# The fifth and sixth chunk loaded earlier, and the dense copies of v made by the scalar engine

## The chip, the cores and the metric

The kernel runs on one core of a Trainium2 chip. The core has a matrix engine (PE, with its weight loads shown as PEld), a vector engine (DVE), a scalar engine (ACT), GpSimd (POOL) and a queue processor (SP) that issues DMA transfers here. Each works through its own instructions in program order, and they wait for each other through semaphores. The metric is device time in microseconds for one run of the kernel; lower is better. Before the change it is 358.11 us, the median of three runs (357.58 to 358.33).

## The reference, cut to what matters

```python
# q, k, v: (8, 8, 576, 64) = batch, head, position, head dimension
scores = q @ k^T / 8                                  # per batch and head
D[n, m] = gamma_h ** (n - m) if n >= m else 0         # gamma_h = 1 - 2 ** (-5 - h)
ret = (scores * D) @ v                                # no softmax
x = ret.transpose(0, 2, 1, 3).reshape(4608, 512)      # tokens by heads
gate = sigmoid(x @ w_gate);  val = x @ w_val          # (4608, 1536) each
out = (gate * val) @ w_out                            # (4608, 512)
```

It is a causal attention with a decay in place of the softmax, so that it can be computed chunk by chunk with a running state; a gated feed-forward layer follows on the same tokens. All inputs are 32-bit floats; the kernel works in bf16 with 32-bit accumulation.

## The kernel before, in words

The 576 positions of a batch are cut into four chunks of 128 and one of 64. A chunk of one batch is a step: 40 in all, numbered from 0, and steps 4, 9, 14 and so on are the half ones. Steps 0 to 3 (the first batch without its tail) take a special path by pairs and read their own loads (`load_pair`). From step 4 on every step goes the same way:

- `load(s)`: three DMA loads on SP, for v, k and q, in pieces of 256 bytes.
- `casts_to(s)`: GpSimd (POOL) scales k and q by the decay tables and casts them to bf16. k goes into `kbd`, a block diagonal tile (three buffers, four instructions for a full chunk), q into `qs` (one instruction). `cross(s)` puts two DMA transposes on SP, k to `kT` and q to `qT`. `cast_v` then writes v to `vbd`, block diagonal, in four copies and, where the chunk isn't the last of its batch, to `vs`, a dense copy, in four more (L252).
- Phase "qk": PE multiplies `kT` and `qT`, and DVE applies the causal mask.
- Phase "pv": PE multiplies scores with `vbd` and adds q times the state, and ACT copies the result, as xT, into the input of the feed-forward part.
- Phases "st0" and "st1": PE multiplies `kbd` and `vs`, which updates the state; DVE casts the state for the next half chunk.

The feed-forward part takes the tokens in blocks of 128 to 512. For each of twelve slices of the hidden layer (an h unit) PE computes gate and value (L457) in PSUM tiles with three buffers, ACT takes the sigmoid, and DVE multiplies. Then PE multiplies by `w_out` (L520), ACT copies the result to an `ob` tile of four, and SP stores it. The attention phases of later steps are spread between these units by `advance`; `run_phase("qk", s)` also issues the loads of step s + 5 and the casts of step s + 2.

All loads share one pool of 18 buffers of 256 KB. SP issues in the order in which the program is written. Every load and transpose counts up one of eight semaphores in turn, and its issue waits for the transfer eight places earlier, so that at most eight are in flight.

The start is written out by hand. SP has pair 0, weights, pair 1, weights (`load_w(f, nf)` loads gate and value weights of nf slices from f), then steps 4 and 5, then `w_out` (`load_wo`). POOL, ACT and DVE cast the weights to bf16 (`cast_w`, `cast_wo`), in the order of the lines around L619 to L660; `h_first(...)` runs the h units of the first block between them. The first multiplication by `w_out` (L664) takes three token tiles at once and has the phases of steps 4 and 5 inside it.

Of the kernel before, what the change touches and what calls it, by code (L numbers as in the profile page):

```python
# [10 lines left out]
BF16 = mybir.dt.bfloat16  # L11
# [5 lines left out]
def kernel(  # L17
# [19 lines left out]
    nc = tc.nc  # L37

    B, H, S, D = q.shape
    NT, DM = out.shape  # L40
    DFF = moe_w_gate.shape[1]
    P = 128
    M = H // 2
    NC = (S + P - 1) // P
    NKC = DM // P
    NFC = DFF // P
# [3 lines left out]
    nat_pool = ctx.enter_context(tc.tile_pool(name="nat", bufs=4))  # L50
# [14 lines left out]
    STEPS = [(b, c) for b in range(B) for c in range(NC)]  # L65
    width = [min(P, S - c * P) for c in range(NC)]
    first_tok = [b * S + c * P for (b, c) in STEPS]
    NS = len(STEPS)
# [3 lines left out]
    loaded = {}  # L72
    parts = {}

    def load(s):
        b, c = STEPS[s]
        n = width[c]
        t0 = c * P
        tiles = []
        for nm, src in (("v", v), ("k", k), ("q", q)):  # L80
            t = ld_pool.tile([P, H, D], FP32, tag="ld", name=f"{nm}32_{s}")
            nc.sync.dma_start(out=t[0:n], in_=src[b, :, t0:t0 + n, :].rearrange("h p d -> p h d"))
            tiles.append(t)
        loaded[s] = tiles
# [11 lines left out]
    def load_w(f, nf):  # L96

        for nm, src in (("g", moe_w_gate), ("v", moe_w_val)):
            for i in range(nf):
                r = NKC // nf  # L100
                t = ld_pool.tile([P, r, nf * P], FP32, tag="ld", name=f"w{nm}32_{f}_{i}")
                nc.sync.dma_start(
                    out=t, in_=src[i * r * P:(i + 1) * r * P, f * P:(f + nf) * P].rearrange("(c p) f -> p c f", p=P))
                parts[nm, f, i] = t

    def load_wo(f):
        t = ld_pool.tile([P, DM], FP32, tag="ld", name=f"wo32_{f}")
        nc.sync.dma_start(out=t, in_=moe_w_out[f * P:(f + 1) * P, :])
        parts["o", f] = t
# [3 lines left out]
    load_pair(1)  # L113
    load_w(2, 2)
    load_w(4, 4)
    load_w(8, 4)
    load(4)
    load(5)
    for f in range(5):
        load_wo(f)  # L120
    LEAD_LOAD = 5
    LEAD_CAST = 2
# [68 lines left out]
    def cast_w(nm, f, nf, i, eng):  # L191
        r = NKC // nf
        at = (slice(None), slice(i * r, (i + 1) * r), slice(f * P, (f + nf) * P))
        eng(out=(wg_sb if nm == "g" else wv_sb)[at], in_=parts.pop((nm, f, i)))  # L194

    on_pool, on_act, on_dve = nc.gpsimd.tensor_copy, nc.scalar.copy, nc.vector.tensor_copy
# [7 lines left out]
    natural = {}  # L204
# [36 lines left out]
    def cast_v(s):  # L241

        b, c = STEPS[s]
        n = width[c]
        v32 = loaded[s][0]
        vb = vbd[s % NB]
        vs = nat_pool.tile([P, 2, M, D], BF16, tag="vs", name=f"vs_{s}")
        for j in range(n // 64):
            for hh in range(2):
                nc.gpsimd.tensor_copy(out=vb[half(hh), j, :, half(hh)], in_=v32[half(j), hh::2, :])  # L250
                if c < NC - 1:
                    nc.gpsimd.tensor_copy(out=vs[half(hh), j], in_=v32[half(j), hh::2, :])  # L252
        natural["vb", s] = vb
        natural["vs", s] = vs

    def cross(s):

# [18 lines left out]
    def half(x):  # L276
        return slice(x * 64, x * 64 + 64)
# [46 lines left out]
    def tile_sv(s, eng):  # L324
        sb = sbd[s % 4]
        for hh in range(2):
            eng(out=sb[half(hh), :, half(hh)], in_=st_tiles[STEPS[s][0]][half(hh)])
        state[s, 1] = sb
# [28 lines left out]
    def phase_qk(s):  # L357
        n = width[STEPS[s][1]]
        nj = n // 64
        kT, qT = turned["k", s], turned["q", s]  # L360
        pt = att_pool.tile([P, M, P], BF16, tag="pt", name=f"pt_{s}")
        qkp = qk_psum.tile([P, M, P], FP32, tag="qk", name=f"qk_{s}")
        for j in range(nj):
            for m in range(M):
                nc.tensor.matmul(qkp[:, m, half(j)], lhsT=kT[:, j, m, :], rhs=qT[:, m, half(j)],  # L365
                                 start=True, stop=True)
        nc.vector.tensor_tensor(out=pt[:, :, 0:n].rearrange("p m (j t) -> p m j t", t=64),  # L367
                                in0=qkp[:, :, 0:n].rearrange("p m (j t) -> p m j t", t=64),
                                in1=tri.unsqueeze(1).unsqueeze(1).to_broadcast([P, M, nj, 64]), op=ALU.mult)
        probs[s] = pt  # L370

    def phase_pv(s):
        b, c = STEPS[s]
        n = width[c]
        t0 = first_tok[s]
        qT = turned["q", s]
        pt = probs.pop(s)
        vb = natural["vb", s]
        pvp = pv_psum.tile([P, M, P], FP32, tag="pv", name=f"pv_{s}")
        for j in range(n // 64):  # L380
            before = state.get((s, j - 1) if j else (s - 1, 1)) if c or j else None
            for m in range(M):
                if before is not None:
                    nc.tensor.matmul(pvp[:, m, half(j)], lhsT=before[:, m, :], rhs=qT[:, m, half(j)],  # L384
                                     start=True, stop=False)
                nc.tensor.matmul(pvp[:, m, half(j)], lhsT=vb[:, j, m, :], rhs=pt[:, m, half(j)],  # L386
                                 start=before is None, stop=True)
        nc.scalar.copy(out=xT[:, :, t0:t0 + n], in_=pvp[:, :, 0:n])  # L388
# [29 lines left out]
    def loads_to(s):  # L418
        while done["ld"] <= min(NS - 1, s):
            load(done["ld"])  # L420
            done["ld"] += 1

    def casts_to(s):
        while done["cast"] <= min(NS - 1, s):
            x = done["cast"]
            cast_k(x)
            cast_q(x)
            cross(x)
            cast_v(x)
            done["cast"] += 1  # L430

    def run_phase(kind, s):
        if kind == "qk":
            loads_to(s + LEAD_LOAD)
            casts_to(s + LEAD_CAST)
            phase_qk(s)
        elif kind == "pv":
            phase_pv(s)
        else:
            phase_st(s, int(kind[2]))  # L440

# [105 lines left out]
    def run(units):  # L547
        for _ in units:
            tick()
# [4 lines left out]
    def h_first(fcs, a, e):  # L554
        run(h_units(gvs, fcs, 0, a, e))
# [63 lines left out]
    pair_out(1, 1, on_dve)  # L619
    pair_st(1, 1)  # L620
    tile_sv(3, on_act)
    for f in (4, 8):
        for i in range(4):
            cast_w("g", f, 4, i, on_pool)
    h_first((2, 3), 0, 2 * P)
    for i in range(2):
        nc.vector.memset(vbd[i], 0.0)
    casts_to(4)
    for f in range(5, 10):
        load_wo(f)  # L630
    casts_to(5)
    for f in range(10, NFC):
        load_wo(f)
    loads_to(6)
    h_first((0, 1, 2), 2 * P, 4 * P)
# [5 lines left out]
    cast_w("v", 4, 4, 3, on_dve)  # L641
    nc.vector.memset(vbd[3], 0.0)
    h_first((4, 5), 0, 4 * P)
    cast_w("v", 8, 4, 0, on_act)
    h_first((6,), 0, 4 * P)
    cast_w("v", 8, 4, 1, on_act)
    cast_w("v", 8, 4, 2, on_dve)
    h_first((7,), 0, 4 * P)
    cast_w("v", 8, 4, 3, on_act)
    h_first((8, 9), 0, 4 * P)  # L650
    cast_wo(0, on_dve)
    cast_wo(1, on_act)
# [70 lines left out]
```

## Time and profile before

| | |
|---|---|
| median of 3 runs | 358.11 us (357.58 to 358.33) |
| the profiled execution | 358.44 us, of which 356.7 us is the span of the profile |
| PE busy | 333.6 us (94%) |
| DVE busy | 162.1 us (45%) |
| ACT busy | 126.8 us (36%) |
| POOL busy | 225.9 us (63%) |
| mean granted PE clock | 0.981 |
| dense copies of v on POOL (L252) | 112 x 399 ns = 44.7 us |

The span runs from the first to the last instruction of one execution; all times inside it are counted from its start. Busy is the time in which an engine has an instruction under way, without its waits. The granted clock is the share of full speed that PE's clock had. In a timeline a row has its start, its length, engine, line, operation, what is written and read, and the number of instructions; square brackets give the idle time before it and what ended it. Such a releaser is inferred from the semaphores: where an instruction waits for several, the one named came last, and if the engine named had long been done, it was another, often a DMA. Rows with "SPq" are issues of transfers, not the transfers.

### The profile page before, as it was taken

The numbers are of one execution on the slowest core, as the hardware profiler recorded it, in microseconds if no ns is written. First come the engines' busy times: TensorE is split into PE (matmuls) and PEld (weight loads), VectorE is DVE, ScalarE is ACT, GpSimd is POOL, SyncE is SP. The second block draws the span as 40 slices with busy tenths as digits, with TensorE's granted clock in tenths as the row PEclk, the third lists the DMA queues.
The fourth block names the chain that finished last, engine by engine and source line by source line (L and its number), as shares of the span: only waits on it lengthen the run. The fifth ranks groups of instructions, "written<-read, shape, count | busy, mean of one in ns | idle before, by whom it ended". The sixth has DMA issues, their size and how long they took to land.

```text
span 356.7 us, 7632 instructions
## 1 busy us (share of the span) xinstructions
PE 333.6 (94%) x2833; PEld 192.2 (54%) x2868; DVE 162.1 (45%) x343; ACT 126.8 (36%) x245; POOL 225.9 (63%) x447
## 2 busy tenths in 40 slices
PE   7899977967699999999999999999999999999996
PEld 3574434755575665655655655555455545554443
DVE  5656412534364653651644663653456345512420
ACT  6766302312233333434323423332333234333321
POOL 7442978999974999489853999879649990000000
PEclk9999989969989999999999999999999999999999
DMA  7999999999999999983985999999699550011002
GB/s 221 315 378 247 230 297 166 207 218 212 189 188 196 209 154 235 208 142 123 179 173 142 163 191 209 197 180 188 145 166 194 130 115 12 0 61 59 2 25 93
DMA packets 169396, 60.27 MB, mean 169 GB/s; under 512 B 152848, under 2 KB 161296, under 8 KB 169360
## 3 DMA queue, kind: packets, MB, share of 16 engines
q1 hardware_dynamic: 169216, 59.66, 82.9%
q8 instruction: 22, 0.36, 0.4%
q14 instruction: 14, 0.11, 0.1%
q10 hardware_dynamic: 144, 0.13, 0.1%
HBM read 37.75 MB, written 9.44 MB: 132 GB/s over the span
## 4 chain that ended last, share of the span: by engine, by line
PE 72%; POOL 14%; DMA 7%; issue 3%; DVE 2%; ACT 1%; SPq 1%; POOLq 0%; ACTq 0%; DVEq 0%
PE h L457 41%; PE op L520 21%; POOL kbd L227 6%; POOL vbd L250 3%; POOL vs L252 2%; POOL qs L237 2%; DMA qT<-qs 2%; DMA q<-in_q_dram 2%; PE qk L365 2%; PE st L398 2%; PE pv L386 2%; PE pv L384 2%; DMA k<-in_k_dram 1%; DMA q32p<-in_q_dram 1%; DVE sbd L404 1%
## 5 line engine op out<-in xcount | busy, mean ns | idle before, releaser
L457 PE MATMUL h<-xT,wv_sb 128*128 128x512 bf16 (+3 forms) x585 | 119.1, 325 | 0.8 <-DVE wv_sb L194 0.4
L457 PE MATMUL h<-xT,wg_sb 128*128 128x512 bf16 (+3 forms) x584 | 119.0, 326 | 0.3
L227 POOL TENSOR_TENSOR kbd<-k,ktab 64x256 bf16<-64x256 f32 x128 | 78.3, 612 | 47.4 <-PE st L398 32.7
L484 DVE TENSOR_TENSOR gv<-g,h 128x512 bf16<-128x512 bf16 (+1 forms) x104 | 65.1, 626 | 69.1 <-PE h L457 65.0
L480 ACT ACTIVATE g<-h 128x512 bf16<-128x512 f32 (+1 forms) x104 | 57.0, 548 | 95.9 <-PE h L457 79.4
L520 PE MATMUL op<-wo_sb,gv 128*128 128x512 bf16 x356 | 84.1, 379 | 0.8
L457 PEld LDWEIGHTS <-wg_sb 128*128 128x128 bf16 x592 | 53.1, 100 | 35.7 <-issue 0.3
L457 PEld LDWEIGHTS <-wv_sb 128*128 128x128 bf16 x592 | 53.1, 100 | 33.3 <-DVE wv_sb L194 0.9
L367 DVE TENSOR_TENSOR pt<-qk,tri 128x512 bf16<-128x512 f32 (+1 forms) x36 | 22.7, 630 | 72.0 <-PE qk L365 71.7
L520 PEld LDWEIGHTS <-gv 128*128 128x128 bf16 x372 | 34.4, 98 | 36.3
L404 DVE CAST sbd<-st 64x256 bf16<-64x256 f32 x112 | 47.0, 420 | 14.9 <-PE st L398 12.5
L250 POOL CAST vbd<-v 64x256 bf16<-64x256 f32 x128 | 50.7, 396 | 4.4
L252 POOL CAST vs<-v 64x256 bf16<-64x256 f32 x112 | 44.7, 399 | 0.0
L492 ACT COPY ob<-op 128x512 f32<-128x512 f32 x35 | 20.3, 587 | 66.3 <-PE op L520 53.6
L237 POOL TENSOR_TENSOR qs<-q,qtab 128x512 bf16<-128x512 f32 (+1 forms) x36 | 37.5, 1041 | 2.8
L388 ACT CAST xT<-pv 128x512 bf16<-128x512 f32 (+1 forms) x36 | 19.4, 538 | 30.2 <-PE pv L386 30.1
L365 PE MATMUL qk<-qT,kT 128*128 128x64 bf16 x256 | 13.6, 195 | 10.4 <-DMA qT<-qs 10.4
L365 PEld LDWEIGHTS <-kT 128*128 128x128 bf16 x256 | 12.7, 99 | 17.1 <-DMA kT<-kbd 9.2
L470 ACT ACTIVATE g<-h 128x256 bf16<-128x256 f32 x32 | 12.3, 384 | 25.3 <-PE h L457 24.2
L398 PEld LDWEIGHTS <-kbd 128*128 128x128 bf16 x224 | 13.5, 100 | 13.2 <-DVE sbd L404 5.1
L386 PE MATMUL pv<-pt,vbd 128*128 128x64 bf16 x256 | 19.5, 194 | 0.0
L384 PE MATMUL pv<-qT,sbd 128*128 128x64 bf16 x228 | 18.5, 195 | 0.1
(66 smaller groups left out, 177.9 us busy)
## 6 DMA issues: line engine op xcount, KB each, us to landing
out_dram<-ob SPq DMA_DIRECT2D x35, 256.0 KB, 2.2
v<-in_v_dram SPq DMA_DIRECT2D x28, 256.0 KB, 3.6
k<-in_k_dram SPq DMA_DIRECT2D x28, 256.0 KB, 4.4
q<-in_q_dram SPq DMA_DIRECT2D x28, 256.0 KB, 5.0
wg<-in_moe_w_gate_dram SPq DMA_DIRECT2D x12, 256.0 KB, 5.6
wv<-in_moe_w_val_dram SPq DMA_DIRECT2D x12, 256.0 KB, 5.5
wo<-in_moe_w_out_dram SPq DMA_DIRECT2D x12, 256.0 KB, 4.0
k32p<-in_k_dram SPq DMA_DIRECT2D x4, 256.0 KB, 4.6
```

The source lines that it names most:

```text
L227: nc.gpsimd.tensor_tensor(out=kn[half(hh), j, :, half(hh)], in0=k32[half(j), hh::2, :], in1=ktab[half(j), c, hh::2].unsqueeze(2).to_broadc ...
L237: nc.gpsimd.tensor_tensor(out=qs[0:n], in0=q32[0:n], in1=qtab[0:n, c, :].unsqueeze(2).to_broadcast([n, H, D]), op=ALU.mult)
L250: nc.gpsimd.tensor_copy(out=vb[half(hh), j, :, half(hh)], in_=v32[half(j), hh::2, :])
L252: nc.gpsimd.tensor_copy(out=vs[half(hh), j], in_=v32[half(j), hh::2, :])
L365: nc.tensor.matmul(qkp[:, m, half(j)], lhsT=kT[:, j, m, :], rhs=qT[:, m, half(j)], start=True, stop=True)
L384: nc.tensor.matmul(pvp[:, m, half(j)], lhsT=before[:, m, :], rhs=qT[:, m, half(j)], start=True, stop=False)
L386: nc.tensor.matmul(pvp[:, m, half(j)], lhsT=vb[:, j, m, :], rhs=pt[:, m, half(j)], start=before is None, stop=True)
L404: nc.vector.tensor_copy(out=sb[half(hh), :, half(hh)], in_=st_tiles[b][half(hh)])
L457: nc.tensor.matmul(out, lhsT=w_sb[:, kc, fc * P:(fc + 1) * P], rhs=xT[:, kc, t0 + a:t0 + e], start=(kc == 0), stop=(kc == NKC - 1))
L480: nc.scalar.activation(out=g[:, 0:n], in_=h1[:, 0:n], func=AF.Sigmoid)
L484: nc.vector.tensor_tensor(out=gvs[some[0]][:, a:e], in0=g[:, 0:n], in1=h2[:, 0:n], op=ALU.mult)
L520: nc.tensor.matmul(opp, lhsT=gvs[fc][:, nb * P:(nb + 1) * P], rhs=wo_sb[:, fc, :], start=(fc == 0), stop=(fc == NFC - 1))
```

## The change

It has three parts. Step 4's loads go ahead of the last block of gate and value weights, `load_w(8, 4)`, on SP, and three tiles of `w_out` are issued before step 4's transposes where it had been five; the others follow in two groups of five and four. On POOL the gate casts of that last weight block move behind the casts of step 4, and the value casts of that block are dealt out to ACT and DVE by turns and begin one h unit later. The dense copies `vs` are taken out of `cast_v` and made by ACT in a function of their own, `cast_dense(s, j)`: the first half of step s + 1 after the pv phase of step s, the second half of step s after its own qk phase. `vs` has two buffers where it had four.

```diff
     load_w(4, 4)
+    load(4)
     load_w(8, 4)
-    load(4)
     load(5)
-    for f in range(5):
+    for f in range(3):
         load_wo(f)
...
-        vs = nat_pool.tile([P, 2, M, D], BF16, tag="vs", name=f"vs_{s}")
         for j in range(n // 64):
             for hh in range(2):
                 nc.gpsimd.tensor_copy(out=vb[half(hh), j, :, half(hh)], in_=v32[half(j), hh::2, :])
-                if c < NC - 1:
-                    nc.gpsimd.tensor_copy(out=vs[half(hh), j], in_=v32[half(j), hh::2, :])
         natural["vb", s] = vb
-        natural["vs", s] = vs
+
+    def cast_dense(s, j):
+
+        if s >= NS or STEPS[s][1] == NC - 1:
+            return
+        if j == 0:
+            natural["vs", s] = nat_pool.tile([P, 2, M, D], BF16, tag="vs", name=f"vs_{s}", bufs=2)
+        for hh in range(2):
+            nc.scalar.copy(out=natural["vs", s][half(hh), j], in_=loaded[s][0][half(j), hh::2, :])
...
             phase_qk(s)
+            cast_dense(s, 1)
         elif kind == "pv":
             phase_pv(s)
+            cast_dense(s + 1, 0)
...
-    for f in (4, 8):
-        for i in range(4):
-            cast_w("g", f, 4, i, on_pool)
+    for i in range(4):
+        cast_w("g", 4, 4, i, on_pool)
     h_first((2, 3), 0, 2 * P)
...
     casts_to(4)
-    for f in range(5, 10):
+    for i in range(4):
+        cast_w("g", 8, 4, i, on_pool)
+    for f in range(3, 8):
         load_wo(f)
     casts_to(5)
-    for f in range(10, NFC):
+    for f in range(8, NFC):
         load_wo(f)
...
     h_first((4, 5), 0, 4 * P)
+    h_first((6,), 0, 4 * P)
     cast_w("v", 8, 4, 0, on_act)
-    h_first((6,), 0, 4 * P)
-    cast_w("v", 8, 4, 1, on_act)
-    cast_w("v", 8, 4, 2, on_dve)
+    cast_w("v", 8, 4, 1, on_dve)
     h_first((7,), 0, 4 * P)
-    cast_w("v", 8, 4, 3, on_act)
+    cast_w("v", 8, 4, 2, on_act)
+    cast_w("v", 8, 4, 3, on_dve)
     h_first((8, 9), 0, 4 * P)
```

## The prediction

> **What bounds the kernel now.** I read first the busy time of each engine in 5 us stretches (columns: PE, PEld, DVE, ACT, POOL busy with counts, granted clock, DMA share, GB/s), then the chain of waits, then the timelines of PE, the transfer queue SP and POOL around the stretch that stood out. Steps are numbered as in the code: the fifth chunk is step 4, the sixth is step 5.
>
> ```profile
> 45.00:50.00 5.00, 3.49 (x13) 1.45 (x13) 0.42 (x1) 0.00 (x0) 4.90 (x10) 0.66 1.16 309
> ...
> 70.00:75.00 5.00, 1.29 (x16) 0.89 (x14) 0.00 (x0) 0.00 (x0) 4.68 (x11) 0.86 1.07 169
> 75.00:80.00 5.00, 5.00 (x64) 4.81 (x62) 3.17 (x9) 1.26 (x3) 4.61 (x8) 0.50 1.16 266
> ...
> 95.00:100.00 5.00, 3.54 (x31) 2.83 (x32) 1.87 (x4) 0.60 (x2) 4.72 (x11) 0.75 1.00 204
> ...
> 110.00:115.00 5.00, 5.00 (x39) 2.81 (x38) 1.66 (x3) 1.84 (x4) 0.54 (x2) 1.00 1.24 170
> ```
>
> From 105 to 350 us PE is busy 243.0 of 245 us at full clock: nothing is to be had there. From 40 to 105 us it is busy 50.95 of 65, so 14.05 us idle, and three times at half clock (46.3 to 49.7, 73.6 to 80.4, 97.5 to 100.9 us). In that stretch POOL is busy 57.2 us and the DMA share is 1.11. Either may be the limit. The chain of waits blames POOL:
>
> ```profile
> PE 72%; POOL 14%; DMA 7%; issue 3%; DVE 2%; ACT 1%; SPq 1%; POOLq 0%; ACTq 0%; DVEq 0%
> ```
>
> PE's timeline shows the long waits: one for POOL's casts of the output weights, then for the transposed q of steps 6, 7 and 10.
>
> ```profile
> 46.51 2.72 PE L664 MATMUL op<-wo_sb,gv 128*128 128x512 bf16 x6 [1.84 <-POOL wo_sb L199]
> ...
> 61.61 0.39 PE L365 MATMUL qk<-qT,kT 128*128 128x64 bf16 x8 [2.17 <-DMA qT<-qs]
> ...
> 96.47 0.39 PE L365 MATMUL qk<-qT,kT 128*128 128x64 bf16 x8 [2.54 <-DMA qT<-qs]
> ```
>
> SP's timeline, start and length of each issue: the loads of step 6, its transposes, and those of step 7.
>
> ```profile
> 48.92 0.57 SPq L82 DMA_DIRECT2D k<-in_k_dram  x1
> ...
> 53.91 1.10 SPq L82 DMA_DIRECT2D q<-in_q_dram  x1
> 56.87 1.24 SPq L261 DMA_TRANSPOSE kT<-kbd  x1
> 58.20 2.12 SPq L265 DMA_TRANSPOSE qT<-qs  x1
> 60.41 0.53 SPq L82 DMA_DIRECT2D v<-in_v_dram  x1
> ...
> 68.43 3.74 SPq L261 DMA_TRANSPOSE kT<-kbd  x1
> 72.26 1.20 SPq L265 DMA_TRANSPOSE qT<-qs  x1
> ```
>
> and POOL's, for the casts that these transposes read:
>
> ```profile
> 45.85 4.53 POOL L199 CAST wo_sb<-wo 128x512 bf16<-128x512 f32 x8
> ...
> 54.19 2.65 POOL L227 TENSOR_TENSOR kbd<-k,ktab 64x256 bf16<-64x256 f32 x4 [1.83 <-DMA k<-in_k_dram]
> ...
> 63.82 1.04 POOL L237 TENSOR_TENSOR qs<-q,qtab 128x512 bf16<-128x512 f32 x1
> ```
>
> Here the chain is misread if taken at its word. Step 7's q was cast by 64.86, its transpose issued at 72.26: POOL was 7.4 us ahead. From 60.41 to 97 us SP issues back to back, over moving data (201 GB/s with the chunks' 256-byte pieces from 62 to 69 us, against 386 with the weights' 2 KB rows from 26 to 28 us). SP waits once, 55.01 to 56.87, for step 6's k cast; and that cast had itself waited 1.83 us for its load. So the limit from 54 to 97 us is the transfer queue, and its clock starts with the landing of step 6's k: issued 48.92, 5.2 us to landing, 54.12.
>
> **The change, part by part.** (a) *Step 4's three loads pass eight weight loads on SP.* They go where the last weight block began, 21.96 instead of 27.36 us. That block's first tile took 5.3 us to land, a step 4 load 6.9 to 7.4: k, issued second at 22.63, lands between 27.9 and 30 instead of 35.5, I take 29. The eight weight tiles land some 3.4 us later: the three loads landed between 32.9 (the last weight tile, 26.67 + 6.2) and 36.3 (28.88 + 7.4).
>
> (b) *POOL's order.* The four wg casts of the last block (27.35, 2.64 us) now stand behind step 4's casts (35.60 to 38.79, so 3.2 us). From 29 these end at 32.2, the four at 34.9. PE first needs them in the ninth h unit, at 35.73 us: cover 0.8 us. Of that block's four wv casts ACT now makes two (0.61 us each), DVE two (0.42 to 0.62), the first a unit later; the last ends near 37.1 against 37.25 for the matmul that reads it (36.60, and the fourth of four in 0.86 us). If this cover is gone PE loses up to 1 us there, which (d) swallows.
>
> (c) *112 dense copies leave POOL*: 112 x 399 ns = 44.7 us, 1.6 us a step (the 6.90 us between the k casts of steps 7 and 8 become about 5.4). In the first stretch four go, step 5's: its casts wait for k5 (30.23 + 8.0 = 38.2), and the casts of wo start at 45.85 - 0.6 - 1.6 = 43.65. PE needs the third of them, POOL's first, at 44.67: the wait of 1.84 us and the half clock behind it (3.41 us, half lost: 1.7) go. Taken alone 3.5 us.
>
> (d) *What is late next.* PE then stands before step 6's scores near 55.5 instead of 59.44, and waits for step 6's transposes, thus for its load. Ahead of that load stand the same transfers as before: w8, steps 4 and 5, twelve wo tiles, two pairs of transposes. Two wo loads move behind step 4's transposes, and two more behind step 5's; all still stand ahead of step 6. So (c)'s 3.5 us are lost again but for what SP gains by the new order. Before, SP spent 2.90 and 2.47 us issuing k5 and q5, and 38.82 to 41.84 on step 4's transposes with little left in flight: from 43.7 to 44.2 us under 70 GB/s moved. Now those transposes can go near 35 us, under weight loads still landing. From 39.3 (q5 landed, 33.22 + 6.1) to 51.7 (the last wo, 47.97 + 3.7) 12.4 us passed; twelve wo tiles of 256 KB at 386 GB/s are 8.2, the four transposes' 590 KB at 201 GB/s 2.9, together 11.1: 1.3 us to gain. With better filling before it, step 6 lands 0 to 3.0 us earlier; I take 1.6, near the 1.3 that rows give. Step 6's POOL casts and everything SP issues to 97 us shift with it, POOL being ahead: **-1.6 us**.
>
> (e) *The clock.* Half clock came in slices of 3.41 us, after slices in which PE was busy 1.37, 0.94 and 1.03 us of 3.41 (42.9, 70.2, 94.1 us), and not after 1.75 and 1.94 (59.95, 80.4 us). The wait before step 6 grows to some 4.5 us and will bring a cold slice, but PE has the wait for step 7 (3.71 us) to lose it in. What counts is the slice after step 10, the last that waits: 3.41 us at half is 1.7 lost. If a shifted wait falls across two slices it goes; step 15's transposed q, which landed 0.9 us before PE used it (124.82 + 3.8, 129.50), then stops PE after some 0.7. Between 0 and 0.7 I take **-0.4**. The Trainium skill (TensorE: Matmul & The Clock Gate, Rules for kernel authors) allows no idle gap over about 3 us; by it the longer wait speaks against this change. Here 2.54 us was enough and 2.17 not, so what a slice holds decides; by the rule one more cold slice would cost 1.7 us, by these rows it is absorbed.
>
> (f) *The copies on ACT.* No row shows them. The nearest is ACT's 64x256 cast out of PSUM, 366 ns; ACT's 128x512 casts took 611 out of SBUF, 586 out of PSUM, so I take 390, ends 366 and 611: 44 us, ACT from 126.8 to 171 us of 357. They queue behind the xT copy (step s+1, first half) and after the scores (second half); behind them wait the next sigmoid, on PE the state matmuls, and on DVE the state's cast. The gaps on ACT cover them: before sigmoids it idles 95.9 us, a gap of 0.6 to 1.2 us each. The tightest place I find is 195.68 to 196.26 (xT), sigmoid at 196.32, state matmul at 197.66: copies to 197.04 leave 0.6 us, and the sigmoid is 0.7 late. A late sigmoid hurts only if PE comes back to its PSUM buffer, three 384-wide halves (0.65 us each) on. Cost 0 to 4.5 us (28 steps x 0.16, if each pair overran its gap by that much); I take **+0.2**, as most pairs fit their gap.
>
> **Sum**: -1.6 - 0.4 + 0.2 = -1.8 us. The profiled execution took 358.44 us (span 356.7 and 1.7 around it), 0.3 above the median 358.11 of the three runs: 356.6 by it, **356.3** by the median.
>
> **Rivals.** *The queue doesn't shift.* Same bytes ahead of step 6, so k lands at 54.1 as before; the POOL gain is waited away, 358.1. For it: DMA share over 1.0 in nearly every slice of this stretch. Against: the slack at 43.7 us. *POOL was the limit after all.* For it the chain, and POOL without a break from 54.2 to 98.8 us. Then steps 6 to 10 each save 1.5, and with (c) about 11 us go: 347. Against it the 7.4 us between cast and transpose. *Slower by ACT*: in the 384- and 512-wide blocks the copies push sigmoids past PE's return; 28 x 0.16 = 4.5 against the 2.0 of (d) and (e): 360.6. It decides from some 0.1 us a step. For it, ACT is strictly in order; against, the gaps. *Slower by the clock*: the longer wait at step 6 moves the pattern so that two more slices after step 10 are cold: -1.6 + 0.2 + 3.4 gives 360.1. *The change does nothing* is the first rival.
>
> **How the numbers follow.** Forecast 0.54 (own range 354.0 to 357.3), no shift 0.18, POOL the limit 0.08, ACT 0.14, clock 0.06. 0.2% (0.72 us) is about what a measurement tells from no change. Faster 0.54 + 0.08 = 0.62, same 0.18, slower 0.20. The low end, 353.4, is -3.0 for the load, -0.7 and -1.0 more for a cold slice gone; the high end 360.3 takes in the clock rival and about half of ACT's. Left out: POOL 0.08, and some 0.07 of ACT.
>
> **What would show it.** Right: step 4's k loads near 22 us, wo casts from about 43.7, no wait for wo_sb, step 6's scores at 59.5 to 61 after a wait over 4 us; steps 7 to 10 each 1 to 2 us earlier with SP still back to back; POOL under 185 us busy, ACT near 170; 105 to 350 us still with PE idle under 3 us. Wrong: step 7's scores before 70 us (POOL was the limit), step 6's k landing at 54 (no shift), or PE waits on ACT's vs or g after 105 us.

## The result, and the profile after

The changed kernel took 359.47 us (median of 4 runs, 358.77 to 359.76) against 358.15 (4 runs, 357.58 to 358.33): a ratio of 1.0037, with a 95% interval of 1.0017 to 1.0056. It is 1.3 us slower. Twelve more runs gave 359.27 against 357.73, a ratio of 1.0047 (1.0023 to 1.0071). The forecast was 1.8 us faster. The profiled execution took 359.24 us, of which 357.5 is span.

The chain of waits of the changed kernel blames POOL less and the transfers more:

```profile
PE 73%; DMA 10%; POOL 9%; issue 3%; DVE 1%; ACT 1%; SPq 1%; POOLq 0%; DVEq 0%; ACTq 0%
```

The changed kernel in the stretches of 5 us that were shown before (columns: PE, PEld, DVE, ACT, POOL busy with counts, clock, DMA share, GB/s):

```profile
45.00:50.00 5.00, 4.83 (x38) 2.37 (x37) 0.56 (x2) 1.88 (x5) 2.20 (x4) 1.00 1.04 242
70.00:75.00 5.00, 2.83 (x20) 1.51 (x18) 0.48 (x2) 0.75 (x2) 4.18 (x8) 1.00 1.22 163
75.00:80.00 5.00, 3.85 (x47) 3.61 (x47) 2.54 (x8) 2.16 (x5) 1.35 (x3) 0.66 1.13 273
95.00:100.00 5.00, 2.86 (x36) 2.69 (x36) 2.04 (x5) 1.39 (x4) 2.61 (x6) 1.00 0.91 201
110.00:115.00 5.00, 5.00 (x40) 2.89 (x39) 2.27 (x5) 2.57 (x6) 0.98 (x2) 1.00 1.25 200
```

PE now runs from 45 to 50 us at full clock, and POOL is busy 2.20 us of it instead of 4.90. But from 70 to 75 PE does 2.83 us, and from 95 to 100 less than before, at full clock instead of 0.75. PE's timeline says what it waits for:

```profile
50.80 1.46 PE L672 MATMUL op<-wo_sb,gv 128*128 128x512 bf16 x6 [0.97 <-POOL wo_sb L199]
...
61.96 0.59 PE L370 MATMUL qk<-qT,kT 128*128 128x64 bf16 x8 [4.23 <-DMA qT<-qs]
...
97.14 0.39 PE L370 MATMUL qk<-qT,kT 128*128 128x64 bf16 x8 [2.77 <-DMA qT<-qs]
```

Step 6's scores start at 61.96 (before 61.61) and step 10's at 97.14 (before 96.47). All that POOL gave back has become a longer wait for step 6. SP's timeline of the changed kernel:

```profile
22.65 1.25 SPq L82 DMA_DIRECT2D k<-in_k_dram  x1
...
49.13 0.54 SPq L82 DMA_DIRECT2D k<-in_k_dram  x1
...
57.42 1.87 SPq L266 DMA_TRANSPOSE kT<-kbd  x1
59.38 1.21 SPq L270 DMA_TRANSPOSE qT<-qs  x1
...
68.59 3.86 SPq L266 DMA_TRANSPOSE kT<-kbd  x1
72.55 1.20 SPq L270 DMA_TRANSPOSE qT<-qs  x1
```

Step 4's k goes out at 22.65, as meant, but step 6's k at 49.13, where it was 48.92. POOL's timeline of the changed kernel:

```profile
43.63 2.34 POOL L199 CAST wo_sb<-wo 128x512 bf16<-128x512 f32 x4
47.23 1.36 POOL L199 CAST wo_sb<-wo 128x512 bf16<-128x512 f32 x2 [1.26 <-DMA wo<-in_moe_w_out_dram]
50.14 1.95 POOL L199 CAST wo_sb<-wo 128x512 bf16<-128x512 f32 x3 [1.55 <-DMA wo<-in_moe_w_out_dram]
...
54.74 2.66 POOL L227 TENSOR_TENSOR kbd<-k,ktab 64x256 bf16<-64x256 f32 x4 [1.87 <-DMA k<-in_k_dram]
```

The casts of wo start at 43.63 us (before 45.85), and then POOL itself waits for the wo tiles, 1.26 and 1.55 us, and as before 1.9 us for step 6's k.

The second place lies past 105 us, where PE had hardly waited before. ACT's timeline of the changed kernel around step 23:

```profile
195.07 0.59 ACT L393 CAST xT<-pv 128x512 bf16<-128x512 f32 x1 [0.62 <-PE pv L391]
195.67 0.82 ACT L259 CAST vs<-v 64x256 bf16<-64x256 f32 x2
196.51 0.49 ACT L487 ACTIVATE g<-h 128x384 bf16<-128x384 f32 x1
```

What DVE does behind that sigmoid, in the same profile:

```profile
197.03 0.55 DVE L491 TENSOR_TENSOR gv<-g,h 128x384 bf16<-128x384 bf16 x1 [1.81 <-ACT g L487]
197.51 0.68 DVE L372 TENSOR_TENSOR pt<-qk,tri 128x512 bf16<-128x512 f32 x1
198.11 0.86 DVE L409 CAST sbd<-st 64x256 bf16<-64x256 f32 x2
```

And PE, which needs that state cast and then step 25's transposed q:

```profile
199.12 0.28 PE L403 MATMUL st<-vs,kbd 128*128 128x64 bf16 x4 [0.49 <-DVE sbd L409]
...
205.58 0.39 PE L370 MATMUL qk<-qT,kT 128*128 128x64 bf16 x8 [0.82 <-DMA qT<-qs]
```

The same places in the kernel before, rows of ACT, DVE and PE:

```profile
195.68 0.59 ACT L388 CAST xT<-pv 128x512 bf16<-128x512 f32 x1 [0.63 <-PE pv L386]
196.32 0.49 ACT L480 ACTIVATE g<-h 128x384 bf16<-128x384 f32 x1
198.12 0.86 DVE L404 CAST sbd<-st 64x256 bf16<-64x256 f32 x2
199.07 0.28 PE L398 MATMUL st<-vs,kbd 128*128 128x64 bf16 x4
```

Two dense copies stand between the xT copy and the sigmoid. The sigmoid is late, so DVE's product is late, the masked scores and the state's cast stand behind it on DVE, and PE's next state matmul waits. PE had been 0.6 us ahead of the kernel before at 195 us; at 199.1 it was level, and after step 25 0.7 behind.

### The profile page after: what moved, and what is told of

Its sections match the earlier page's. It is cut to its first block, busy times and chain, and to the rows that moved or that the text cites. A ratio compares the mean times of both kernels' runs of the same rounds, so it can differ in the third digit from the quotient of the medians.

```text
span 357.5 us, 7682 instructions
## 1 busy us (share of the span) xinstructions
PE 334.3 (94%) x2868; PEld 191.7 (54%) x2868; DVE 162.9 (46%) x344; ACT 171.2 (48%) x356; POOL 187.5 (52%) x335
## 3 DMA queue, kind: packets, MB, share of 16 engines
q1 hardware_dynamic: 169216, 59.66, 84.0%
## 4 chain that ended last, share of the span: by engine, by line
PE 73%; DMA 10%; POOL 9%; issue 3%; DVE 1%; ACT 1%; SPq 1%; POOLq 0%; DVEq 0%; ACTq 0%
PE h L464 43%; PE op L527 20%; POOL kbd L227 5%; DMA qT<-qs 3%; POOL vbd L249 2%; PE qk L370 2%; PE st L403 2%; POOL qs L237 2%; DMA kT<-kbd 2%; DMA k<-in_k_dram 2%; PE pv L391 2%; DMA q32p<-in_q_dram 1%; PE pv L389 1%; DMA v<-in_v_dram 1%; DMA wo<-in_moe_w_out_dram 1%
## 5 line engine op out<-in xcount | busy, mean ns | idle before, releaser
L527 PE MATMUL op<-wo_sb,gv 128*128 128x512 bf16 x372 | 85.5, 379 | 0.0
L259 ACT CAST vs<-v 64x256 bf16<-64x256 f32 x112 | 45.1, 403 | 1.8
L370 PE MATMUL qk<-qT,kT 128*128 128x64 bf16 x256 | 13.7, 196 | 12.0 <-DMA qT<-qs 12.0
L403 PE MATMUL st<-vs,kbd 128*128 128x64 bf16 x224 | 15.8, 193 | 3.6 <-DVE sbd L409 3.0
```

The costliest lines, as they stand in the source:

```text
L259: nc.scalar.copy(out=natural["vs", s][half(hh), j], in_=loaded[s][0][half(j), hh::2, :])
L403: nc.tensor.matmul(st_tiles[b][:, m, :], lhsT=natural["k", s][:, j, m, :], rhs=natural["vs", s][:, j, m, :], start=(c == 0 and j == 0 and ...
L527: nc.tensor.matmul(opp, lhsT=gvs[fc][:, nb * P:(nb + 1) * P], rhs=wo_sb[:, fc, :], start=(fc == 0), stop=(fc == NFC - 1))
```

## The experiments

The theories keep the numbers that the expectations give them. Theory 1: up to 97 us the transfer queue sets the pace, so the change gains nothing there, and it loses at two late places, by ACT's copies at step 23 and by step 25's transposes. Rivals: ACT's copies alone (2), the moved loads (3), half clock (4), chance (5). Theories 6, 7 and 8 came with later runs.

All kernels of one group ran beside runs of the kernel before on the same chip. What follows uses a table of times taken from the profile of each, one execution each; L means the landing of a transposed q, and the last column is the time from step 15's scores to step 39's.

| kernel | L step 6 | L step 10 | third store | L step 25 | 15 to 39 |
|---|---|---|---|---|---|
| before | 61.57 | 96.42 | 191.19 | 204.88 | 186.4 |
| changed | 61.92 | 97.10 | 190.51 | 205.54 | 187.8 |
| changed, again | 61.36 | 96.29 | 190.32 | 205.16 | 187.6 |
| order only | 62.18 | 96.74 | 190.60 | 204.71 | 186.8 |
| copies only | 61.15 | 95.66 | 189.06 | 203.96 | 187.7 |
| copies earlier | 61.46 | 96.31 | 190.21 | 205.39 | 188.4 |
| no copies | 60.88 | 95.54 | 189.02 | 202.67 | 186.3 |
| changed, lead 4 | 61.75 | 92.68 | 188.10 | 202.50 | 187.3 |
| before, lead 4 | 61.30 | 91.33 | 185.85 | 199.16 | 186.4 |
| before, lead 3 | 62.81 | 90.51 | 185.35 | 199.38 | 187.3 |
| changed, 24 more on ACT | 62.43 | 96.86 | 190.74 | 205.05 | 187.3 |
| before, 60 more on ACT | 60.87 | 95.79 | 189.94 | 204.25 | 187.0 |
| before, 64 bytes | 61.94 | 96.20 | 190.42 | 204.27 | 186.5 |
| before, 32 bytes | 57.23 | 88.97 | 182.67 | 196.17 | 186.2 |
| changed, 32 bytes | 59.38 | 92.75 | 186.17 | 200.19 | 187.3 |
| before, 32 bytes, lead 3 | 59.43 | 86.94 | 181.40 | 194.77 | 186.1 |
| changed, stores on ACT | 64.36 | 96.72 | | 198.98 | 188.1 |
| changed, 24 more on ACT, new tile | 58.22 | 90.91 | 184.48 | 198.46 | 187.3 |
| before, 60 more on ACT, new tile | 58.95 | 92.44 | 185.57 | 199.35 | 186.5 |
| copies earlier, 24 more, new tile | 58.26 | 91.53 | 186.75 | 200.10 | 186.9 |

"Lead 4" and "lead 3" are loads four and three steps ahead on SP instead of five; "new tile", "32 bytes" and "64 bytes" are explained with the runs that have them. "Third store" is when SP issues the third of three output stores, for which it stands still with step 24's and 25's transposes behind them. A single execution can lie well off its kernel's median: those of "no copies", "before, lead 4" and "before, 32 bytes" took 1.7 to 2.2 us less than it, that of "before, 32 bytes, lead 3" 2.4 us more.

### The two parts alone

Order only: the dense copies go back to POOL, the rest of the change stays.

```diff
+                if c < NC - 1:
+                    nc.gpsimd.tensor_copy(out=vs[half(hh), j], in_=v32[half(j), hh::2, :])
...
-            cast_dense(s, 1)
...
-            cast_dense(s + 1, 0)
```

> The new order of loads and casts alone: the dense copies stay on POOL, between its copies into vbd, as before. Theory 1 (the queue, then two late pinches): up to 97 us PE follows the landings of the transposed q, and the same bytes stand ahead of them, so step 10's scores stay at 96 to 97 us; the loss comes from the copies, through ACT at step 23 and through POOL, which being ahead lets step 25's transposes be issued into loads in flight. So no loss here: 357.6 to 358.6 us, no wait on sbd at 199 us, qT of step 25 lands at 204.5 to 205. Rival 2 (ACT's copies alone): 358.1. Rival 3 (the moved loads): the loss is here already, 359.2 to 359.8. Rival 4 (half-clock slices): the time follows the mean granted clock, 1.7 us for each slice of 3.41 us, whatever the kernel.

Measured: 358.40 us against 358.26, ratio 1.001 (0.9994 to 1.0026). No loss to speak of, as theory 1 expected, and step 25's q landed at 204.71 us, in its range.

Copies only: `cast_dense` put into the kernel before, its loads and casts untouched.

> The copies alone: dense copies of v on ACT, two a phase, loads and casts in the order of before. Theory 1: 359.0 to 359.8 us, with the wait of 0.5 us on sbd near 199 us and qT of step 25 landing near 205.5. Rival 2: 359.5. Rival 3: 358.1. Rival 4: no rule but the clock's.

Measured: 358.04 against 358.26, ratio 0.9999 (0.9983 to 1.0015). Theory 1 and rival 2 both missed here: neither part alone costs anything that can be measured. The profile has both late waits all the same (0.48 us for the state's cast, 0.69 for step 25's q), and step 15 to step 39 takes 187.7 us, 1.3 more than before; what made up for it is that step 15's scores came at 127.4 us instead of 129.5. The order-only run rules out rival 3, that the moved loads alone are the loss (359.2 to 359.8 us by it).

### The copies at another place

```diff
         elif kind == "pv":
             phase_pv(s)
-            cast_dense(s + 1, 0)
+            if s == PAIRED or STEPS[s][1] == NC - 1:
+                cast_dense(s + 1, 0)
+                cast_dense(s + 1, 1)
         else:
             phase_st(s, int(kind[2]))
+            cast_dense(s + 1, int(kind[2]))
```

and the call behind the scores is taken out.

> The changed kernel with ACT's copies a step earlier: the pair for step s+1 goes behind the state matmuls of step s (first and second half) instead of behind the xT copy and the scores; where step s has no state, both pairs go behind its second product as one. This takes the pair from between the xT copy and the sigmoid at 195.67 us. Theory 1: the wait on sbd at 199 us goes, PE comes to step 25 some 0.6 us earlier and waits there for the transposed q, which lands at 205.5 all the same: 359.0 to 359.6 us. Rival 2: 358.0 to 358.4. Rival 3: 359.5.

Measured: 358.94 against 358.26, ratio 1.0019 (1.0001 to 1.0036), just under the range of theory 1 and above that of rival 2. In this kernel's profile PE's wait at 199 us is gone, and step 25 takes all of it back:

```profile
205.44 0.39 PE L370 MATMUL qk<-qT,kT 128*128 128x64 bf16 x8 [1.72 <-DMA qT<-qs]
```

So two costs run side by side there, ACT's and the queue's, and taking one away shows the other.

### The stores on another queue

```diff
-        stores.append([hold, r0, ob])
+        nc.scalar.dma_start(out[r0:r0 + P, :], ob)
```

> The changed kernel with the output stores issued by ACT right behind its copy into ob, not by SP; SP then no longer stands from 184.9 to 190.9 us behind three stores, with step 24's transposes (cast by 184) behind them. Theory 1: step 24's transposes are issued near 184 to 186 and step 25's by 199, its q lands before 202, PE's wait of 0.8 us there is gone, and the time is 0.7 to 1.5 us below that of the changed kernel, 357.5 to 358.6 us. If the end does not hang on that landing, the time stays. The issues cost ACT some 0.36 us each by SP's rows for its own issue of a store; if that pushes the sigmoids, up to 1 us is lost.

Measured: 359.28 against 357.73, ratio 1.0039 (1.0019 to 1.0058); theory 1 had 357.5 to 358.6 and missed. The same row of this kernel's profile has no wait any more:

```profile
205.06 0.40 PE L370 MATMUL qk<-qT,kT 128*128 128x64 bf16 x8
```

Step 25's q landed at 198.98, 6 us early, yet 15 to 39 took 188.1 us and the time stayed. The waits for the state's cast (0.48 and 0.56 us) remained, and issuing the stores made ACT's own work late elsewhere (PE waited 0.54 us for a sigmoid at 140.8 and 3.3 us for xT at 61.0). The end did not hang on that landing alone, as I had put it.

### The changed kernel again, and without any dense copy

> The changed kernel once more, beside the same runs of before as the next three. In the six profiles so far the span was the landing of step 25's transposed q plus 151.8 to 152.1 us (before 204.88 + 151.8, after 205.54 + 152.0), and the stretch from the third output store of the block before (191.19 and 190.51 us) to that landing was 13.7 and 14.1 us with the dense copies on POOL (before, order only) and 14.9, 15.0 and 15.2 with them on ACT (copies only, changed kernel, copies earlier). Theory 1, now put so: the end hangs on that landing; the change gains about 1.4 us between step 10 and the third store (a slice at half clock that no longer comes) and loses 0.7 before step 10 and 1.3 after the store. It expects 358.6 to 359.6 us, so slower by 0.3 to 1.3, and the stretch at 14.8 to 15.3 us. Rival 5: order alone and copies alone each cost nothing (358.40 and 358.04 against 358.26), so the first four runs of the changed kernel were high by chance: 357.9 to 358.6.

Measured: 359.27 against 357.73. The loss is real and rival 5 (chance) falls. The stretch from the third store to the landing was 14.8 us. Rival 4 (half clock) falls too: of the runs of the changed kernel, those with a mean granted clock above 0.987 took 358.8 us on average (5 runs) against 357.8 before (24), the others 359.8 (11) against 358.1 (34). At like clocks it is 1.0 to 1.7 us slower.

Without copies, `vs0` being one tile of zeros that every step reads:

```diff
-        for hh in range(2):
-            nc.scalar.copy(out=natural["vs", s][half(hh), j], in_=loaded[s][0][half(j), hh::2, :])
+        if s < NS:
+            natural["vs", s] = vs0
```

> The changed kernel with the dense copies of v left out on every engine: the state matmuls read one tile of zeros, so the states are zero and the output lacks the part of earlier chunks from step 4 on; matmuls, loads and transposes are the same in number. It tells what lengthens the stretch from the third store to the landing of step 25's q. If it is ACT's copies (their reads beside the transfers, or the sigmoid they push back), the stretch falls to 13.7 to 14.1 us and the time to 357.5 to 358.3. If it is that POOL, rid of the copies, is done earlier and the transposes go into loads in flight, the stretch stays at 14.8 to 15.3 and the time at 358.5 to 359.3, though no wait on sbd near 199 us is left. In both cases step 10's scores stay at 96 to 97.2 us.

Measured: 358.14 against 357.73, ratio 1.0011 (0.999 to 1.0032), stretch 13.7 us, 15 to 39 186.3 us. So the copies cost 1.1 us by the medians in a kernel that has everything else of the change (the means differ by 1.4, with a 95% interval of 0.5 to 2.3), and without them the change is worth nothing, though POOL is as free as in the changed kernel. That POOL's relief lets transposes go too early is not what lengthens the stretch: POOL has no dense copies here and the stretch is short, in the one profile that was taken.

### Fewer loads ahead on SP

```diff
-    LEAD_LOAD = 5
+    LEAD_LOAD = 4
```

> The changed kernel with the loads four steps ahead instead of five, so that the three loads of one step fewer stand ahead of each step's transposes on SP; bytes, copies and casts as they are. Theory 1: the transposes of steps 7 to 10 are issued up to 3.5 us earlier (three loads of 256 KB at 200 to 240 GB/s), step 7's scores at 72.5 to 73.5 instead of 75.2, step 10's at 92 to 95 instead of 97.1, and the time is 355 to 357.5 us. If POOL were the limit up to 97 us the casts would hold the transposes and the time stays at 359.5. If loads come late later on (steps 24 to 28, where the queue is full again) some of it is lost: not over 1 us.

> The kernel before with the loads four steps ahead instead of five; no other part of the change. It tells whether the change is worth something once fewer loads stand ahead of the transposes on SP. Theory 1: with the copies still on POOL its casts for steps 7 to 10 (71.8, 77.3 and 81.9 us for steps 8 to 10) are late by about what the queue gains, so the gain is smaller than the 2.1 us that the changed kernel had from it: 356.3 to 357.7 us. If POOL's relief is worth nothing at all, it equals the changed kernel with four: 355.7 to 356.5.

Measured: the changed kernel with four 356.17 against 358.26, ratio 0.9941 (0.9918 to 0.9963); the kernel before with four 355.25 against 357.73, ratio 0.9915 (0.9884 to 0.9947). SP's timeline of the changed kernel with four:

```profile
62.73 0.87 SPq L82 DMA_DIRECT2D v<-in_v_dram  x1
63.64 0.63 SPq L82 DMA_DIRECT2D k<-in_k_dram  x1
64.32 0.63 SPq L82 DMA_DIRECT2D q<-in_q_dram  x1
65.06 1.95 SPq L266 DMA_TRANSPOSE kT<-kbd  x1
67.10 1.22 SPq L270 DMA_TRANSPOSE qT<-qs  x1
```

Step 7's q goes out at 67.10 instead of 72.55, with three loads fewer ahead of it; it had been cast by 64.05 in both. Step 10's q lands at 92.7 in the changed kernel instead of 97.1 and at 91.3 in the kernel before instead of 96.4. So up to 97 us the limit is the order on the transfer queue, and one number moves it by more than the whole change did. The kernel before gained 2.5 us and ended below the range that I had given it; the changed kernel gained more against its own 359.3 to 359.5 us, some 3.2 (in runs of different groups), and with four it is still about 0.9 us the slower of the two. Whether the copies on POOL hold anything back can't be read from such a difference.

### More instructions on ACT, and a surprise

Two theories were left for the stretch from the third store to step 25's q: 13.3 to 14.1 us in the four profiles so far with no copies on ACT, 14.4 to 15.2 in the five with them in SP's queue order (that is, without the stores on ACT). ACT's copies may lengthen it as such. Or it is a transfer of the program itself, 8 KB on queue q14. Such transfers came at nearly the same counts of ACT's instructions in each profile, about 126 apart, so I take them to be ACT's; with 112 copies more one of them fell into just that stretch. The transfers of the changed kernel from 197.5 to 205.5 us, by queue:

```profile
q8 instruction: 1, 0.02, 0.8%
q14 instruction: 1, 0.01, 0.4%
```

In the kernel before, the same stretch has a row for q8 alone. To move that transfer, one-column copies were added:

```diff
                 nc.scalar.activation(out=g[:, 0:n], in_=h1[:, 0:n], func=AF.Sigmoid)
+                for _ in range({1408: 1, 1792: 1}.get(t0, 0)):
+                    nc.scalar.copy(out=tiny, in_=lnscale)
```

with `tiny` a new tile of one column; in the kernel before, the rule is `{1024: 2, 1408: 2, 1792: 1}`.

> The changed kernel with 24 one-column copies more on ACT, one behind each sigmoid of the blocks at rows 1408 and 1792 (136 to 184 us), their result unused. What it is for: in every profile the instruction queue q14 moves 8 KB for ACT about when ACT is at its 65th, 193rd, 319th and 444th instruction; with the dense copies on ACT the 319th is reached at 198 to 202 us, between the landings of step 24's and step 25's q, with them on POOL at 253 to 259. 24 more instructions bring that transfer to about 187 us, when SP stands behind the output stores. Theory 6 (the program's own transfer in that stretch delays step 25's transposes): the stretch from the third store to the landing of step 25's q falls from 14.8 to 15.2 us to 13.3 to 14.1, PE's wait for it to under 0.3, and the time to 358.3 to 358.9 us where the changed kernel has 359.3 against 357.7 to 358.2 of before. Theory 7 (ACT's copies as such lengthen it): the stretch stays at 14.8 to 15.2 and the time at 359.1 to 359.8.

> The kernel before, dense copies on POOL, with 60 one-column copies on ACT: two behind each sigmoid of the blocks at rows 1024 and 1408, one in the block at 1792. They bring ACT's 319th instruction from 258.9 to about 199 to 202 us. Theory 6: the stretch from the third store to the landing of step 25's q grows from 13.7 to 14.6 or more, PE waits 0.8 to 1.5 us there, and the time is 358.6 to 359.4 us. Theory 7: no dense copy is on ACT, so the stretch stays at 13.3 to 14.1 and the time at 357.7 to 358.3.

> Copies a step earlier and the 24 one-column copies together. Theory 6 with the sigmoid at 195.67 us as the second cost: both prices of the copies go, neither the wait on sbd near 199 us nor one over 0.3 us for step 25's q is left, steps 15 to 39 take 186.3 to 187.0 us as with the copies on POOL, not 187.6 to 188.4, and the time is 357.7 to 358.5 us. Theory 7: 358.8 to 359.4.

Measured: 353.72, 351.57 and 353.45 us against 358.76, ratios 0.9871 (0.9833 to 0.9909), 0.9795 (0.9766 to 0.9825) and 0.9863 (0.9831 to 0.9895). No theory had that: more work, 5 to 7 us less. The gain was there before the first added instruction ran, step 6's q landing at 58.2 to 59.0 us. The new tile is all that comes earlier. It takes 32 bytes per partition, and every tile behind it moves: the loads' tiles began at 111584, which is 32 modulo 64 and 224 modulo 256, and now at 111616, a multiple of 512. So these runs tell nothing of the two theories. The next two have the copies of the first two, with the result written to a tile that is there already.

> The changed kernel with 24 more one-column copies on ACT in the blocks at rows 1408 and 1792, written to a tile that is there already, so that no tile moves. Theory 6 (the program's transfer for ACT): the stretch from the third store to the landing of step 25's q is 13.3 to 14.1 us instead of 14.8 to 15.2; PE, held up by the sigmoids all the same, gains at most 0.6: 358.6 to 359.3 us. Theory 7 (the copies as such): 14.8 to 15.2 us, 359.1 to 359.9.

> The kernel before with 60 more one-column copies on ACT, to a tile that is there already. ACT's 319th instruction then comes at 199 to 203 us instead of 259. Theory 6: the stretch from the third store to the landing of step 25's q grows from 13.3 to 14.1 us to 14.5 or more, and the time by 0.5 to 1.0 us. Theory 7: 13.3 to 14.1 us, and the time stays within 0.4 of that of before.

Measured: 359.75 and 359.17 against 358.2, ratios 1.0047 (1.0024 to 1.007) and 1.0034 (1.0013 to 1.0056). The stretch was 14.3 us in both, between the two ranges. With the program's transfer moved out it is some 0.6 us shorter in the changed kernel, with it moved in about as much longer in the kernel before: half of the difference of 1.2 us. But these are single profiles, and profiles of like kernels differ by 0.8, so neither theory is shown. The stretch does not decide the time: the changed kernel was no faster for it. The kernel before was about 1 us slower with 60 more instructions on ACT, so their own time can't be told from that of the transfer.

### The place of the tiles

```diff
     nc.scalar.activation(out=warm, in_=lnscale, func=AF.Sigmoid)
+    tiny = consts.tile([P, 1], FP32, name="tiny")
+    nc.gpsimd.memset(tiny, 0.0)
```

and with `[P, 16]` for 64 bytes.

> The kernel before with one more constant of 4 bytes, which takes 32 bytes per partition: the loads' tiles begin at 111616 instead of 111584, so at a multiple of 64 bytes, and everything behind moves with them. Theory 8 (where the tiles lie sets how fast the transfers of 256-byte pieces go): 351 to 353.5 us against 357.7 to 358.8, with step 6's q landing at 58 to 59.5 instead of 61.6 and step 10's scores at 91 to 93. If the extra ACT instructions did it, the time stays at 357.7 to 358.8.

> The changed kernel with the same 32 bytes. Theory 8: 352 to 355 us. The price of ACT's copies after step 15 (steps 15 to 39 took 186.3 to 187.0 us with the dense copies on POOL, 187.6 to 188.4 with them on ACT) does not hang on the layout, so it stays 0.5 to 1.5 us slower than the kernel before with 32 bytes; if the change's loss were one of the transfers alone, the two are equal within 0.4.

> The kernel before with one more constant of 64 bytes per partition: the loads' tiles begin at 111648, again 32 modulo 64, as at 111584 before. If it is the multiple of 64 bytes that makes the transfers faster, nothing is gained: 357.5 to 359 us, step 6's q lands at 60.5 to 62.5. If any other place does as well, 351 to 353.5 us and 57 to 59.5.

Measured: the kernel before with 32 bytes 351.38 against 358.2, ratio 0.9809 (0.9777 to 0.9842); the changed kernel with 32 bytes 353.49, ratio 0.9863 (0.9837 to 0.9888); the kernel before with 64 bytes 357.93 against 357.98, ratio 1.0003 (0.9983 to 1.0022). Moved by 64 bytes the tiles are no better off than where they were, so it is not the move itself that helps, but the place; these three places are all that were tried. The constant's memset on POOL is not the cause either: the three kernels with a new tile above have none. The change itself leaves the loads' tiles where they were and moves what lies behind them by two `vs` buffers, 2048 bytes, a multiple of 512, so the place of the tiles is no part of its loss.

The pair with 32 bytes also shows what ACT's copies cost where the transfers are faster and PE hardly waits for step 25's q. All that PE waits for between 105 and 345 us, in the changed kernel with 32 bytes:

```profile
PE st L405 <- DVE sbd L411: 1.2, 3, 0.6
PE st L405 <- POOL kbd L229: 0.2, 1, 0.2
```

and in the kernel before with 32 bytes:

```profile
PE qk L367 <- DMA qT<-qs: 0.2, 1, 0.2
```

1.2 us for the state's cast: the two longest of the three waits, 0.48 and 0.56 us, are for casts held up on DVE behind a product that waits for a late sigmoid. The change loses 2.1 us by the medians in this layout (from 5 and 6 runs, whose times overlap); 15 to 39 gives 1.1 of that (187.3 against 186.2). The rest lies before step 15, where single profiles differ too much to place it.

### Three steps ahead, alone and with the 32 bytes

> The kernel before with the loads three steps ahead. With four it took 355.25 us against 357.73. If the queue's order is the limit up to 97 us and POOL is not, step 7 to 10's transposes go another 3.5 us earlier where their casts allow it; but with the copies on POOL the casts of steps 8 to 10 end at 71.7, 77.3 and 81.9 us and those transposes were issued at 75.1, 83.1 and 88.5 with four steps: 3.4 to 6.6 us to gain at most. Steps 24 to 28, where loads are late, pay up to 2. 353 to 356.5 us.

> The kernel before with the constant of 32 bytes and the loads three steps ahead. Apart the two took 351.4 and 352.6 us against 358.2 to 358.8. Both work on the same waits, those for the transposed q of steps 6 to 11; with the 32 bytes PE still waited 1.8, 2.0, 2.1 and 1.5 us there, so at most some 5 us more are to be had, less what the casts of steps 7 to 10, which the order with three waits for, hold back: 347.5 to 351 us.

Measured: 352.62 against 358.76, ratio 0.9838 (0.981 to 0.9867); with the 32 bytes 345.88 against 357.98, ratio 0.9662 (0.9626 to 0.9697). That is 12 us less than the kernel before and some 13.5 less than the changed one, with three lines: `LEAD_LOAD = 3` and the constant with its memset. Alone the two had gained 6.1 and 6.8 us, together 12.1: they nearly add up, and the time is below the range that I had given.

## Why the prediction was wrong

(a) *Step 4's loads.* Right: issued at 22.65 us, k landed at 29.8 (predicted 29).

(b) *POOL's order.* Right in the outcome, but barely: the four gate casts of the last block ended at 35.59 (predicted 34.9), and PE's ninth unit starts at 35.65 without a wait. The cover was 0.06 us, not 0.8.

(c) *The copies leave POOL.* Right where it was local: the casts of wo began at 43.63 us, predicted 43.65. POOL's busy time fell by 38.4 us (225.9 to 187.5), not 44.7. The wait for wo_sb did not vanish (0.97 us at 50.80): with POOL early, the wo tiles' landing was late next.

(d) *What is late next: here the first term failed.* PE came early to step 6 and waited 4.23 us, as predicted; that SP would have step 6's load 1.6 us earlier was wrong. I had reckoned that from the landing of step 5's q to that of the last wo tile 11.1 us would do instead of 12.4. It took 13.2 in the changed kernel. With the tiles where they were, it took 12.5 to 13.3 in the seven other profiles with the new order of loads and 12.1 to 13.0 in the six with the old one (12.4 in the kernel before): the new order gained nothing there, and step 6's k landed no earlier with it (at 54.6 us on average, 54.3 with the old one). The term that was mis-sized is the four transposes, 2.9 us by the rate of the chunk loads: the last wo tiles landed 0.7 us apart, so twelve of them take 8.4, and 3.7 to 4.9 are left. The packets agree: taken in the order of issue, those of the four transposes kept the 16 engines busy for an estimated 3.8 us in the kernel before and 4.4 in the changed one. The pause near 44 us that I took for slack is when step 4's transposes landed in the kernel before (44.3 and 44.7 us). Step 6's k landed at 54.7, which I had named as the sign of no shift, and the rival "the queue doesn't shift" is what happened up to 97 us.

(e) *The clock.* Predicted -0.4. The mean granted clock was 0.986 before (the 58 runs of the first two groups) and 0.984 after (16 runs). A cold slice of 3.41 us is 0.005 of that mean, so there was none fewer. The two first profiles showed 0.981 and 0.990, and the next of the changed kernel 0.986: a pattern of slices read from one execution did not hold. In the changed kernel's first profile half clock began at 61.4 and 75.1 us, in the waits of 4.23 and 2.34 us before steps 6 and 7, and not after the 2.77 us before step 10, so the length of the wait alone did not decide there either, nor does the rule of about 3 us that the prediction quotes (it stands in that page's section Why this matters for your kernels): 2.34 and 2.77 us are both within it.

(f) *The copies on ACT: the second term that failed.* The price of one, 390 ns, was right (403 measured), and so was the tightest place, the pair at 195.67 us, and even the size of the delay there. What failed is "most pairs fit their gap", and the sentence that a late sigmoid hurts only if PE comes back to its PSUM buffer. I had named DVE's state cast as waiting behind the copies and then priced PSUM alone. The path that cost runs over DVE: a late sigmoid, a late product, the state's cast behind it, PE's state matmul. Of the ten profiles with the copies on ACT the mean from step 15 to step 39 was 187.6 us, of the ten others 186.5: 1.05 us, in place of +0.2. The ends that I gave (0 to 4.5) held it.

With (d) and (e) at nothing and (f) at 1.0 to 1.4 the sum is near the +1.3 to +1.5 measured. The rival "slower by ACT" had the sign and the late sigmoid, but its path was PE coming back to the PSUM buffer, not DVE, and its price 4.5 us. What stays open: copies alone in the order of before cost nothing by the median (358.04), so part of the loss seems to need both parts of the change at once (by the means the two parts alone fall short of the whole by 1.2 us, with a standard error of 0.5). Its place is before step 15, whose scores came at 127.4 us in the copies-only profile and at 128.8 and 128.6 in the two of the changed kernel; why was not shown.

## What to carry to other kernels

An engine that the chain blames may be waiting on the same transfer queue as PE: before pricing its relief, ask what the queue must move first, and price each kind of transfer by its own rows. Then try the cheapest change of order on that queue; here one constant was worth 2 to 6 us where moving work between engines was worth -1.3. And an engine that is 36% busy is not free: what counts is whether the new work fits in front of the next instruction that someone waits for, along every engine behind it.

## What the runs showed of the hardware

The place of tiles in the on-chip memory decided more than anything else tried. The same 59.66 MB on SP's queue took the following shares of the 16 engines' span. Before (span 356.7 us):

```profile
q1 hardware_dynamic: 169216, 59.66, 82.9%
```

before with 64 bytes (span 356.1 us):

```profile
q1 hardware_dynamic: 169216, 59.66, 84.2%
```

before with 32 bytes (span 348.0 us):

```profile
q1 hardware_dynamic: 169216, 59.66, 74.0%
```

That is 296, 300 and 258 us per engine: with the loads' tiles at a multiple of 512 bytes the same data took 13 to 14% less transfer time than at 224 or 32 modulo 256. The five other kernels with this place took 253 to 258 us. Most of that is in the packets of 256 bytes, which the chunk loads and the transposes move: 221, 227 and 187 us per engine, all other sizes together 75, 73 and 70. The Trainium skill (DMA: Bandwidth & Descriptors, How a descriptor splits into AXI transactions) says that a transaction must start at a multiple of 256 bytes; by that a piece of 256 bytes that begins off such a multiple takes two transactions in place of one. The runs agree with that in direction. They don't separate 64, 256 and 512 bytes. Taken in the order of issue, the packets of the k loads fell from an estimated 21 ns to 18 (from the kernel before to that with 32 bytes) and those of the k transposes from 37 to 29, so both gain; which of the moved tiles is behind it, what a transpose reads or what it writes, they don't show.

The program's own transfers show up as queues of their own (q8, 16 KB at a time, and q14, 8 KB). In the changed kernel one of 8 KB came when ACT was at about its 65th, 193rd, 319th and 444th instruction, and with more instructions on ACT the third of these moved: from 201 us to 187 with 24 more in the changed kernel, from 259 to 201 with 60 more in the kernel before.
